# Attention and two-layer network on one Trainium2 core: units from 18 on scored in three chunks of 128 keys and a shared rest of 64

## Chip, core and metric

The kernel runs on one core of one Trainium2 chip. The metric is device time in microseconds from start to end of one execution; several executions are timed and the median is given. The profile is one more execution, recorded by the hardware profiler.

The engines of the core: TensorE (PE; its weight loads are listed apart as PEld), VectorE (DVE), ScalarE (ACT), GpSimd (POOL) and SyncE (SP). GpSimd and SyncE also issue the DMAs here, each in the order of its own queue. Each engine runs its instructions in program order, and semaphores hold it where it needs another's result.

## The reference

```python
batch, n_heads, seq, head_dim = (8, 12, 448, 64)
n_tokens, d_model, d_ff = (3584, 768, 2048)

scores = scale * np.matmul(q, k.transpose(0, 1, 3, 2))
scores = scores - np.max(scores, axis=-1, keepdims=True)
attn = np.exp(scores)
attn = attn / (np.sum(attn, axis=-1, keepdims=True) + 1e-09)
attn_out = np.matmul(attn, v)

x = attn_out.transpose(0, 2, 1, 3).reshape(B * S, H * D)
h = x @ w_in
g = np.maximum(0.01 * h, h)
out = g @ w_out
```

Inputs and output are float32; the kernel computes in bfloat16 with float32 sums.

## The kernel before

**Units, chunks, bursts.** Attention is cut into `NU` = 48 *units*: a unit is one batch and a pair of heads. A unit's 448 keys are cut into `NSC` = 4 *chunks* of `SC` = 112 keys. The scores of a chunk (`scores`, L284) are two matmuls, one for each head of the pair: 64 rows (the head dimension) of the array each, on the upper and the lower half of the rows, with the keys as weights and all 448 queries as the moving operand. They fill a *slot*, two banks of PSUM; there are three (`slots`). ScalarE turns a slot into exponentials in `e_sb` (`expo`, L296), 896 a partition; no maximum is taken off. A *burst* (`burst`, L819) is the scores of the next three chunks, whatever units they belong to, one slot each, and their exponentials.

**Rows.** When a unit's four chunks are there, `rows` (L790) multiplies by v: for each head and each 112 queries, four matmuls with the exponentials as weights and 65 columns of v moving (64 and a column of ones, which gives the sum), 32 in all, into one slot. VectorE takes the reciprocal of the sums and multiplies; x is then turned by a transposing DMA on SP's queue (or, for the units in `X_PE`, by TensorE) into `xT`.

**The supply of a unit.** GpSimd issues the loads of q, k and v, two units at a time, with a cast to bfloat16 on the way (`load_soft`, L140); the loads use rooms in not yet used weight buffers first, then `ld_pool` with two buffers a kind. GpSimd then copies q and k of a unit into one of four `qkb` buffers and v into one of four `v_sb` buffers (`cast`, L165). Up to unit 14 (`NPE` = 15) TensorE transposes q and k (`transposes`, L265); from unit 15 on one transposing DMA on SP's queue does it (`dma_transposes`, L257), into one of `NQ` = 4 buffers `qkT`. SP's queue also carries the turns of x (`x_transposes`, L320) and all stores of the output.

**The network.** Tokens are cut at `cuts` into seven blocks. For each block come the hidden layer (`hidden`, L464, matmuls L489; for the first block `head` and `neck`) and the output layer (`second` with `block_pair`, L544, matmuls L561). Both use a scheme that replaces eight half-size products by seven, with sums and differences on VectorE (`mix_x_part`, `mix_h` and others).

**The order.** Python writes out the whole order of the instructions. During `head`, `neck` and `second`, `place` (L878) decides after every few products what to put between them: a transpose, a burst, or a unit's rows. It has a small model of time: `model["now"]` for TensorE, `model["act"]` for ScalarE, when each slot comes free, when each unit's exponentials are ready. `plan` (L875) says how many bursts each of the seven `second` stages takes; `need` says how many units must be done for each block. During `hidden` two of the three slots serve the products, no burst is placed, and the loop at L999 puts rows at every fourth step. `advance` (L768) issues turns, copies and loads as their lookahead allows (a turn of unit u when `u < chunk // NSC + NQ`, a copy when `u < to["turn"] + 2`); `feed` (L857) does that in the first block.

Of the kernel before, what the change touches and what calls it, by code (L numbers as in the profile page):

```python
# [16 lines left out]
def kernel(  # L17
# [9 lines left out]
    nc = tc.nc  # L27
# [10 lines left out]
    NU = B * HP  # L38
    scale = 1.0 / float(D) ** 0.5
# [10 lines left out]
    ld_pool = ctx.enter_context(tc.tile_pool(name="ld", bufs=2))  # L50
# [32 lines left out]
    v_sb = [v_pool.tile([SC, 2, NSC, VL], BF16, name=f"v{i}") for i in range(NV)]  # L83
# [3 lines left out]
    e_sb = [exp_pool.tile([SC, EL + P - SC], BF16, name=f"e{i}") for i in range(NE)]  # L87
# [4 lines left out]
    qkT = [qk_pool.tile([P, QL + P - SC], BF16, name=f"qkT{i}") for i in range(NQ)]  # L92
# [27 lines left out]
    qkb = [cast_pool.tile([SC, 2, NSC, 2, D], BF16, name=f"qkb{i}") for i in range(4)]  # L120
# [4 lines left out]
    for t, n in ((h_mix, 2), (w_in_mix, 9), (w_mix, 9)):  # L125
        t = t.rearrange("p x k n -> p (x k n)")
        for j in range(n):
            rooms.append(t[:SC, ts(j, 4 * NSC * D)].bitcast(F32).rearrange("p (h so d) -> p h so d", h=2, so=NSC))

    def room(x):  # L130

        return rooms.pop(0) if rooms else ld_pool.tile([SC, 2, NSC, D], F32, name="f" + "qkv"[x])

    def half(t, i=None):

        t = t.rearrange("p h so d -> p (h so d)").bitcast(BF16)
        t = t.rearrange("p (u h so d) -> p u h so d", u=2, h=2, so=NSC)
        return t if i is None else t[:, i]

    def load_soft(u, n, which):  # L140
        b, hp = divmod(u, HP)
        for x in which:
            t = room(x)
# [8 lines left out]
    def load_one(u, x, queue):  # L152
        b, hp = divmod(u, HP)
        t = room(x)
# [10 lines left out]
    def cast(u, parts=(0, 1, 2), by=nc.gpsimd.tensor_copy):  # L165
        if u >= NU:
            return
        for x in parts:
            f = raw[u].pop(x)
            if x < 2 and u not in qk_sb:  # L170
                qk_sb[u] = qkb[u % len(qkb)]
            t, n = (qk_sb[u][:, x], D) if x < 2 else (v_sb[u % NV], D)
            if f.dtype == BF16 and by == nc.gpsimd.tensor_copy:
                t, f, n = t.bitcast(F32), f.bitcast(F32), D // 2
            by(t.rearrange("p so h d -> p h so d") if x < 2 else t[:, :, :, :n], f)  # L175
# [60 lines left out]
    for t in e_sb:  # L236
        nc.vector.memset(t[:, EL:], 0.0)
    for t in qkT:
        nc.vector.memset(t[:, QL:], 0.0)
# [14 lines left out]
    def turn(dst, src):  # L254
        nc.sync.dma_start_transpose(out=dst.rearrange("p (c s) -> p c s", s=SC), in_=src)
# [9 lines left out]
    def transposes(u, bank=None):  # L265
        if u >= min(NPE, NU):
            return
        for parts in ((1,), (0,)) if u == 0 else ((0, 1),):
            tr = turn_tile(bank)
            for i in parts:  # L270
                for so in range(NSC):
                    nc.tensor.transpose(  # L272
                        tr[:, i, ts(so, SC)], qk_sb[u][:, i, so], ident[:SC, :SC]
# [9 lines left out]

# [751 lines left out]
```

## Time and profile before

| | |
|---|---|
| median of 3 runs | 383.2 us (383.15 to 383.98) |
| the profiled execution, its own time | 382.9 us |
| its span, first to last instruction | 381.1 us |
| instructions | 10099 |
| mean granted clock of TensorE | 1.000 |
| score matmuls (L289), 64 rows x 448 columns | 384 |
| exponentials (L298), 112 x 896 | 192 |
| attention times v in `rows` (L799), 112 rows x 65 columns | 1344 |
| output-layer matmuls of 384 columns (L561): with w_out and h, w_mix and h, w_mix and h_mix | 448, 216, 112 |
| loads of q, k, v in `ld_pool` (two units each) | 19 each |
| transposing DMAs of q and k, of x | 33, 44 |
| DMA packets, moved | 92798, 46.98 MB |

How such lines are read: a group is "line engine op, out<-in, shapes xcount | busy us, mean ns of one | idle time of the engine just before them, and what ended most of it". A wait is "engine, line <- what it waited for: us in total, times, longest". A timeline row is "start us, us, engine line op, tiles, shapes xcount", several like instructions merged. A window row is "from:to length, busy (xcount) ..., granted clock, DMA share, GB/s". Matmul ends are modelled, so TensorE is best read from start to start.

### The profile page before, as it was taken

How to read it: one execution, taken by the hardware profiler on the slowest of the kernel's cores; microseconds unless marked ns; L12 is line 12 of the kernel's file. 1: busy time of each engine (PE TensorE's matmuls, PEld its weight loads, DVE VectorE, ACT ScalarE, POOL GpSimd, SP SyncE). 2: the span in 40 equal slices, each digit the busy share in tenths (PEclk: the TensorE clock that was granted, in tenths of full speed). 3: DMA queues.
4: the chain of work that ended last, by engine and by line, in shares of the span. 5: the costliest groups of instructions: out<-in, count | busy, mean ns of one | idle time of the engine just before them, and what ended most of it. 6: DMA issues, size and time to landing. Idle time of an engine off the chain costs nothing.

```text
span 381.1 us, 10099 instructions
## 1 busy us (share of the span) xinstructions
PE 374.3 (98%) x4123; PEld 261.4 (69%) x4123; DVE 232.1 (61%) x510; ACT 265.1 (70%) x392; POOL 111.7 (29%) x223
## 2 busy tenths in 40 slices
PE   8899999999999999999999999999999999999996
PEld 6665658756598565986558865688656895668854
DVE  3662767776666645666466674665745665474753
ACT  6997885866768777588766777668777687717700
POOL 5966663452326211251121512213322000000000
PEclk9999999999999999999999999999999999999999
DMA  8999999999898945999458994679949630331023
GB/s 157 168 202 203 200 190 207 181 124 168 133 179 81 139 108 99 165 112 123 118 89 148 107 144 89 118 131 99 159 71 147 122 61 0 109 77 33 1 83 84
DMA packets 92798, 46.98 MB, mean 123 GB/s; under 512 B 51408, under 2 KB 89424, under 8 KB 92752
## 3 DMA queue, kind: packets, MB, share of 16 engines
q0 software_dynamic: 37536, 22.24, 45.6%
q1 hardware_dynamic: 54480, 23.44, 35.5%
q10 hardware_dynamic: 736, 0.66, 0.6%
q8 instruction: 32, 0.52, 0.6%
q14 instruction: 14, 0.11, 0.1%
HBM read 45.61 MB, written 11.01 MB: 149 GB/s over the span
## 4 chain that ended last, share of the span: by engine, by line
PE 94%; ACT 2%; DVE 2%; DMA 1%; issue 0%; DVEq 0%
PE g L561 34%; PE g L489 14%; PE sc L489 14%; PE sc L289 11%; PE sc L799 10%; PE g L370 4%; ACT e L298 2%; PE g L656 2%; PE g L272 1%; DMA hmix<-in_k_dram 1%; PE g L308 1%; PE sc L370 1%; DVE x L806 1%; PE g L335 0%; DVE qkT L278 0%
## 5 line engine op out<-in xcount | busy, mean ns | idle before, releaser
L298 ACT ACTIVATE e<-sc 112x896 bf16<-112x896 f32 x192 | 162.6, 920 | 45.2 <-PE sc L289 45.0
L561 PEld LDWEIGHTS <-h 128*128 128x128 bf16 x680 | 61.2, 98 | 48.0 <-issue 14.1
L561 PE MATMUL g<-w_out_sb,h 128*128 128x384 bf16 x448 | 87.2, 327 | 0.0
L478 ACT ACTIVATE h<-c 128x512 bf16<-128x512 f32 (+1 forms) x72 | 43.5, 611 | 24.0 <-DVE c L504 14.0
L489 PEld LDWEIGHTS <-w_in_sb 128*128 128x128 bf16 x576 | 54.3, 98 | 6.0
L289 PE MATMUL sc<-qkT 64*128 64x448 bf16 x384 | 50.0, 353 | 1.7 <-ACT e L298 0.6
L175 POOL COPY v<-fv 112x256 f32<-112x256 f32 x38 | 16.2, 425 | 117.3 <-PE sc L799 98.6
L799 PEld LDWEIGHTS <-e 112*128 112x128 bf16 x1344 | 46.5, 97 | 4.4
L799 PE MATMUL sc<-v,e 112*128 112x65 bf16 x1344 | 47.7, 193 | 0.0
L489 PEld LDWEIGHTS <-w_in_mix 128*128 128x128 bf16 x432 | 41.1, 98 | 4.1
L566 DVE COPY o<-g 128x384 f32<-128x384 f32 x53 | 29.4, 554 | 22.5 <-PE g L561 22.2
L561 PE MATMUL g<-w_mix,h 128*128 128x384 bf16 (+1 forms) x224 | 41.8, 325 | 0.0
L289 PEld LDWEIGHTS <-qkT 64*128 64x128 bf16 x384 | 15.8, 94 | 28.9 <-issue 19.6
L569 DVE TENSOR_TENSOR o<-o,g 128x384 f32<-128x384 f32 x42 | 23.2, 552 | 18.1 <-PE g L561 16.3
L805 DVE RECIPROCAL rec<-sc 112x8 f32<-112x8 f32 x42 | 8.7, 208 | 36.9 <-PE sc L799 36.7
L806 DVE TENSOR_TENSOR x<-sc,rec 112x512 bf16<-112x512 f32 x42 | 29.0, 691 | 1.5
L489 PE MATMUL g<-xT,w_in_sb 128*128 128x256 bf16 (+1 forms) x216 | 28.5, 268 | 0.0
L489 PE MATMUL sc<-xT,w_in_sb 128*128 128x256 bf16 (+1 forms) x216 | 28.5, 268 | 0.0
L175 POOL COPY qkb<-fq 112x256 f32<-112x256 f32 x38 | 16.7, 441 | 32.8 <-DMA fq<-in_q_dram 32.8
L175 POOL COPY qkb<-fk 112x256 f32<-112x256 f32 x38 | 17.4, 458 | 27.5 <-DMA fk<-in_k_dram 27.5
L561 PE MATMUL g<-w_mix,hmix 128*128 128x384 bf16 x112 | 21.7, 327 | 0.0
L489 PE MATMUL g<-x_mix,w_in_mix 128*128 128x256 bf16 (+1 forms) x144 | 19.0, 268 | 0.0
(107 smaller groups left out, 455.0 us busy)
## 6 DMA issues: line engine op xcount, KB each, us to landing
fq<-in_q_dram POOLq DMA_DIRECT2D x19, 224.0 KB, 7.5
fk<-in_k_dram POOLq DMA_DIRECT2D x19, 224.0 KB, 8.9
fv<-in_v_dram POOLq DMA_DIRECT2D x19, 224.0 KB, 6.0
w_in_sb<-in_moe_w_in_dram POOLq DMA_DIRECT2D x4, 768.0 KB, 12.2
w_out_sb<-in_moe_w_out_dram POOLq DMA_DIRECT2D x4, 768.0 KB, 17.9
out_dram<-o SPq DMA_DIRECT2D x7, 336.0 KB, 3.0
out_dram<-o SPq DMA_DIRECT2D x8, 288.0 KB, 3.3
out_dram<-o SPq DMA_DIRECT2D x7, 240.0 KB, 2.9
```

Source lines behind the costliest of these rows:

```text
L175: by(t.rearrange("p so h d -> p h so d") if x < 2 else t[:, :, :, :n], f)
L289: nc.tensor.matmul(ps[:, j, :S], t[j * D:(j + 1) * D, S + c * SC:S + c * SC + P], t[j * D:(j + 1) * D, :S], start=True, stop=True,)
L298: nc.scalar.activation(e[:, :, c, :], sc_t.pop((u, c))[:SC, :, :S], AX.Exp, scale=scale)
L370: nc.tensor.matmul(open_t[m][:, :n], w_in_sb[:, kk, ts(m, P)], xT[:, kk, at:at + n], start=(fresh and kk == kks[0]), stop=(kk == KD - 1),)
L478: nc.scalar.activation(hs[:, m:m + 2, cols], x.rearrange("p (m t) -> p m t", m=2), AX.Prelu, alpha=0.01)
L489: nc.tensor.matmul(ps[:, j * nh:(j + 1) * nh], w[:, kk, ts(j, P)], x[:, kk], start=(first and j == 0 and kk == 0), stop=(kk == KH - 1), sk ...
L561: nc.tensor.matmul(ps[:, cols], x[:, m], w[:, m], start=(first and m == 0), stop=(m == MH - 1), skip_group_check=True,)
L566: by(o[:, at], ps[:, :NW])
L569: nc.vector.tensor_add(o[:, at], o[:, at], ps[:, :NW])
L799: nc.tensor.matmul(ps[:, j, qc, :D + 1], e[:, at:at + P], vt[:, j, c, :D + 1], start=(c == 0), stop=(c == NSC - 1),)
L805: nc.vector.reciprocal(rec, ps[:SC, :, :, D:D + 1])
L806: nc.vector.tensor_mul(x_t[u].rearrange("p q j d -> p j q d"), ps[:SC, :, :, :D], rec.to_broadcast([SC, 2, NSC, D]))
```

## The change

From unit 18 on (`WIDE = 3 * HP`) a unit's keys are cut into three chunks of 128 and 64 left over. A burst is then the three chunks of one unit. The 64 keys left over of both heads share one matmul, the *rest* (`rest`): the weights are 128 rows (the two heads' 64 dimensions) by 128 columns (64 keys of each head), with zeros where a head's rows meet the other head's keys; the moving operand is q of both heads; the exponentials are one instruction of 448. A rest takes a slot of its own, and is placed by `place` or, in the hidden-layer stages, in the place of rows.

`rows` becomes, for each 112 queries, three matmuls a head over 128 keys, and one over the shared rest whose moving operand is v of both heads, 130 columns: 28 matmuls a unit.

To hold this, q, k and v buffers get 128 partitions; k and v loads of these units become three DMAs, with memsets that set the zeros in the buffers' first use; the transposing DMA takes 128 rows in place of 112 (q with zero rows). `qkb` has three buffers for four, so a copy waits for the turn of three units before; in `feed` a copy is put off until that turn stands in the program (unit 17's comes behind unit 14's). In the hidden-layer stages a turn is issued at most at every sixth step. `plan` goes from 46 bursts to 36.

```diff
+    WIDE = 3 * HP
+    NWC = S // P
+    REST = S - NWC * P
...
-    qkT = [qk_pool.tile([P, QL + P - SC], BF16, name=f"qkT{i}") for i in range(NQ)]
+    qkT = [qk_pool.tile([P, 2 * NSC * P], BF16, name=f"qkT{i}") for i in range(NQ)]
+    qkb = [cast_pool.tile([P, 2 * NSC, 2, D], BF16, name=f"qkb{i}") for i in range(3)]
...
+    def load_wide(u, x):
...
+        src = (q, k, v)[x][b, 2 * hp:2 * hp + 4]
+        nc.gpsimd.dma_start(
+            out=t[:, :, :, :NWC].rearrange("p u h so d -> p (u h) (so d)"),
+            in_=src[:, :NWC * P].rearrange("h (p so) d -> p h (so d)", so=NWC),
+        )
+        for j in range(2):
+            own, other = (slice(y * REST, (y + 1) * REST) for y in (j, 1 - j))
+            if u < WIDE + 4:
+                nc.gpsimd.memset(t[other, :, j, NWC], 0.0)
+            nc.gpsimd.dma_start(out=t[own, :, j, NWC], in_=src[j::2, NWC * P:].rearrange("u r d -> r u d"))
...
     def load_soft(u, n, which):
...
+            if x > 0 and u >= WIDE:
+                load_wide(u, x)
+                continue
...
     def cast(u, parts=(0, 1, 2), by=nc.gpsimd.tensor_copy):
...
+                assert u < len(qkb) or u - len(qkb) in gone, u
...
+            if x == 0 and WIDE <= u < WIDE + len(qkb):
+                nc.gpsimd.memset(qk_sb[u][96:, :NSC], 0.0)
...
+            if x == 2 and WIDE <= u < WIDE + NV:
+                for j in range(2):
+                    nc.gpsimd.memset(v_sb[u % NV][(1 - j) * REST:(2 - j) * REST, j, NWC, D:D + 1], 0.0)
...
         if NPE <= u < NU:
-            turn(qkT[u % NQ][:, :QL], qk_sb[u].rearrange("p i so h d -> p (i so h d)"))
+            gone.add(u)
+            rows_of, s = (P, P) if u >= WIDE else (SC, SC)
+            turn(qkT[u % NQ][:, :2 * NSC * s], qk_sb[u][:rows_of].rearrange("p so h d -> p (so h d)"), s)
...
+    def rest(u):
+
+        ps = next_slot()[:, 0, :S]
+        nc.tensor.matmul(ps, qkT[u % NQ][:, (2 * NSC - 1) * P:2 * NSC * P], q_of(u), start=True, stop=True)
+        at = 2 * NWC * S
+        nc.scalar.activation(e_sb[u % NE][:, at:at + S], ps, AX.Exp, scale=scale)
...
-    def advance(hold=False, due=NU):
+    def advance(hold=False, due=NU, turns=True):
...
-        if u < min(NU, chunk // NSC + NQ, to["cast"]) and (u <= due or not hold):
+        if turns and u < min(NU, scored() + NQ, to["cast"]) and (u <= due or not hold):
...
             for qc in range(NSC):
+                b, y = divmod(2 * qc, NSC)
+                for j in range(2):
+                    for c in range(NWC):
+                        at = (j * NWC + c) * S + qc * SC
+                        nc.tensor.matmul(
+                            ps[:, b, y + j, :D + 1], e[:, at:at + P], vt[:, j, c, :D + 1],
+                            start=(y + j + c == 0), stop=False, skip_group_check=True,
+                        )
+                at = 2 * NWC * S + qc * SC
+                nc.tensor.matmul(
+                    ps[:, b, y:y + 2, :D + 1], e[:, at:at + P], vt[:, :, NWC, :D + 1],
+                    start=False, stop=True, skip_group_check=True,
+                )
...
     def burst(lazy=0):
...
+        if todo[0][0] >= WIDE:
+            assert todo[0][1] == 0
+            owed_rest.append(todo[0][0])
...
-        if r < 3 or g >= NPE:
+        if (r < 3 or g >= NPE) and (u < len(qkb) or u - len(qkb) in gone):
...
-    plan = [9, 8, 8, 8, 8, 5, 0]
+    plan = [8, 7, 6, 6, 6, 3, 0]
...
-            if want > done and state < 2 and turned(last) and not blocked and len(slots) == 3 and all(
+            if want > done and state < 2 and turned(last) and not blocked and not owed_rest and len(slots) == 3 and all(
...
+            if calm and owed_rest and at[0] <= now + 0.05:
+                t = slots[0]
+                u = set_rest()
+                model["act"] = max(model["act"], now + 0.25) + 0.5
+                free[id(t)] = model["act"] + 0.15
+                ready[u] = model["act"] + 0.1
+                model["now"] = now + 0.19
+                continue
...
         for step, _ in enumerate(hidden(i)):
-            advance()
-            if step % 4 == 2 and (i > 1 or step > 2) and NSC * (rows_done + 1) <= chunk:
+            advance(turns=step % 6 == 0)
+            if step % 4 == 2 and owed_rest:
+                set_rest()
+            elif step % 4 == 2 and (i > 1 or step > 2) and rows_done < scored():
                 rows()
```

More of the change, by code (lines that the diff above doesn't have):

```diff
@@ L119 @@
     qk_sb = {}
-    qkb = [cast_pool.tile([SC, 2, NSC, 2, D], BF16, name=f"qkb{i}") for i in range(4)]
+    gone = set()
     rooms = []
@@ L153, in load_one @@
         b, hp = divmod(u, HP)
-        t = room(x)
+        t = room(x)[:SC]
         queue.dma_start(
@@ L921, in place @@
             u = to["pe"]
-            if first and full and state == 0 and u < min(NPE - 1, to["cast"] - 1) and u <= chunk // NSC + 1 and model["act"] <= now + 0.6:
+            if first and full and state == 0 and u < min(NPE - 1, to["cast"] - 1) and u <= scored() + 1 and model["act"] <= now + 0.6:
                 transposes(u)
@@ L948, in second @@
                 if x % 4 == 0:
-                    advance(i + 1 < NR and rows_done >= need[i + 2] - 3 and not all(summed), (chunk + 3 * left - 1) // NSC)
+                    advance(i + 1 < NR and rows_done >= need[i + 2] - 3 and not all(summed), at_chunk(chunk + 3 * left - 1)[0])
                 if c or x:
```

106 lines of the change are left out of this document (69 added, 37 removed).

## The prediction

> **What bounds the kernel now.** I read the page first (busy time, slices, chain), then TensorE's timeline and stage windows, and last the queues that feed it.
>
> ```profile
> PE 374.3 (98%) x4123; PEld 261.4 (69%) x4123; DVE 232.1 (61%) x510; ACT 265.1 (70%) x392; POOL 111.7 (29%) x223
> ```
> ```profile
> PE 94%; ACT 2%; DVE 2%; DMA 1%; issue 0%; DVEq 0%
> ```
>
> TensorE is busy 98% of the span and makes 94% of the chain that ends last. The waits of its matmuls ask whether that is real work or waiting on others:
>
> ```profile
> PE sc L289 <- ACT e L298: 0.6, 2, 0.4
> ```
> ```profile
> PEld L289 <- DMA qkT<-qkb: 0.6, 2, 0.3
> ```
>
> In the whole span the score matmuls (L289) waited 0.6 us for a score slot and 0.6 us for turned q and k. So the time is a sum of TensorE's matmuls, and what the change does to that sum is the forecast, provided that nothing late gets in front of it. The rows that price its pieces are from the first stage after the second token block:
>
> ```profile
> 131.71 0.49 PE L561 MATMUL g<-w_out_sb,h 128*128 128x384 bf16 x2
> 132.03 0.81 PE L561 MATMUL g<-w_mix,hmix 128*128 128x384 bf16 x4
> 132.78 0.74 PE L289 MATMUL sc<-qkT 64*128 64x448 bf16 x6
> 133.45 0.82 PE L561 MATMUL g<-w_mix,hmix 128*128 128x384 bf16 x4
> 134.11 0.49 PE L561 MATMUL g<-w_out_sb,h 128*128 128x384 bf16 x2
> 134.44 1.14 PE L799 MATMUL sc<-v,e 112*128 112x65 bf16 x32
> 135.41 1.14 PE L561 MATMUL g<-w_out_sb,h 128*128 128x384 bf16 x6
> ```
>
> The second column of a merged row holds the tail of its last matmul, so prices are read from start to start. Rows of attention times v (L799) cost 135.41 - 134.44 = 0.97 us for 32 matmuls, and the products beside them (L561) 0.163 us each: six of them fill the usual 0.98. Ahead of the burst the four from 132.03 take 0.75 instead of 0.65, and the burst itself 0.67. A burst thus costs more than its own row. Two stages with the same products and the same attention rows give its full price; the windows are of all TensorE, then of L289, L799 and L561 alone:
>
> ```profile
> 124.19:152.65 28.46, 28.46 (x291) 1.00 0.72 114
> 314.73:340.73 26.00, 26.00 (x272) 1.00 0.20 49
> ```
> ```profile
> 124.19:152.65 28.46, 5.93 (x48) 1.93 (x48) 1.00 0.72 114
> 314.73:340.73 26.00, 3.71 (x30) 1.11 (x30) 1.00 0.20 49
> ```
> ```profile
> 124.19:152.65 28.46, 4.55 (x128) 4.44 (x128) 1.00 0.72 114
> 314.73:340.73 26.00, 4.55 (x128) 4.44 (x128) 1.00 0.20 49
> ```
> ```profile
> 124.19:152.65 28.46, 20.36 (x112) 9.91 (x111) 1.00 0.72 114
> 314.73:340.73 26.00, 19.73 (x112) 10.16 (x112) 1.00 0.20 49
> ```
>
> Both have 112 products and 128 attention-times-v matmuls, and TensorE has no gap in either (the last three numbers of a row are the granted clock, the mean share of the DMA engines and GB/s). The first has 48 score matmuls, the second 30: three bursts more, and 2.46 us more. A burst therefore costs 0.82 us. Clock 1.00 throughout, so no term hangs on the clock.
>
> **The change, part by part.** Units 18 to 47 are 30 units. Before, they take four chunks each, 120 chunks, 40 bursts of three. Afterwards each takes one burst and one rest, so 30 bursts. The plan's sum falls accordingly, from 46 to 36.
>
> Removed: 10 bursts x 0.82 = **-8.2 us**.
>
> Added: 30 rests, each one matmul of 128 rows, 128 columns of weights and 448 moving columns. The nearest row has exactly this shape, w_in against 448 tokens:
>
> ```profile
> 35.04 1.14 PE g L370 x6
> ```
>
> 1.14 / 6 = 0.19 us, so 30 x 0.19 = **+5.7 us**. Lower end: nothing shows 448 columns cheaper, so 0.19. Upper end: a burst's three pairs stream 3 x 0.19 = 0.57 of its 0.82, which leaves 0.25 for passing from whole-array matmuls to 64-row ones and back; a rest that paid all of it would cost 0.44, or 7.5 us more over 30. I take 0.19, because the rest uses all 128 rows as the products do, and L799 to L561 changes weights and slots with no loss. If a rest comes right behind a burst, it only takes over the exit that the next product paid.
>
> The Trainium skill, "TensorEngine Tiling (Array Packing)", Key Properties, says that changing the tiling mode drains TensorE. That fits the 0.25 of a burst, and would put nothing on a rest. The Trainium skill, "TensorE: Matmul & The Clock Gate", Back-to-back issue gap, gives a sustained 81 ns a matmul at 128 columns and 131 ns at 512. By it a rest would cost about 0.12 (an estimate between those two figures), and the sum would be 2 us lower. The row of the same shape has 0.19, and the row decides.
>
> Attention times v: per unit 32 matmuls of 65 columns become 24 of 65 and 4 of 130, the same 2080 columns. Below, a price by instruction: 28 x 30.3 ns = 0.85 us, -0.12 a unit or -3.6 in all. Above, a price by column alone: 0.97, no gain. The two rows between which it lies, 65 columns at 30.3 ns and 448 at 190, give 0.417 ns a column and a fixed 3.2 ns. Then 130 columns take 57.4 ns, and the unit 24 x 30.3 + 4 x 57.4 = 957 ns. I take that: 0.013 x 30 = **-0.4 us**. Contracting 128 rows for 112 changes no column count.
>
> On ScalarE a unit's exponentials go from four of 896 to three of 896 and one of 448:
>
> ```profile
> L298 ACT ACTIVATE e<-sc 112x896 bf16<-112x896 f32 x192 | 162.6, 920 | 45.2 <-PE sc L289 45.0
> L634 ACT ACTIVATE h<-g 128x448 bf16<-128x448 f32 x14 | 7.7, 550 | 2.1 <-PE g L370 1.7
> ```
>
> 162.6 / 192 = 0.85 us, so 3.39 becomes 2.54 + 0.55 at most: 0.3 us less a unit. ScalarE idles 45 us in front of the exponentials waiting for scores, so this is worth nothing, but it removes a cover that could have failed. Score slots are used five times a unit before (four chunks, one rows) and after (three, the rest, one rows). The planner now counts a rest at 0.5 on ScalarE, about that price. In the hidden-layer stages, where one slot is left, a rest goes two products after the stage's start and pushes the rows back by four products (some 2.6 us); those rows are for a later token block. Cost on the path: nothing.
>
> Loads: each k and v load of two units becomes three issues on GpSimd's queue, and the first two of each kind also get two memsets.
>
> ```profile
> L144 POOL DMA_DIRECT2D fk<-in_k_dram x19 | 13.4, 704 | 2.7 <-DMA w_out_sb<-in_moe_w_out_dram 1.9 <-DMA w_in_sb<-in_moe_w_in_dram 0.5 <-issue 0.3
> ```
> ```profile
> POOL v L175 <- PE sc L799: 98.6, 22, 10.0
> ```
> ```profile
> fk<-in_k_dram POOLq DMA_DIRECT2D x19, 224.0 KB, 8.9
> ```
> ```profile
> 0.74 0.20 POOL masks.py:197 MEMSET c<- 128x128 bf16 x1 [0.29 <-POOLq L1019]
> ```
>
> Four more issues a pair of units are 4 x 0.70 = 2.8 us, 42 us over 15 pairs, and the 19 memsets at 0.2 another 4. GpSimd works 111.7 of 381 us and spends 98.6 more waiting for v buffers, which covers it. Bytes grow by nothing, but a load's pieces grow from 448 (112 partitions x 4 heads) to 512 + 256, so a k load lands in 8.9 us if bytes count and in 8.9 x 768/448 = 15.3 if pieces do. I take 12; two buffers of a pair each last four units, which is 32 us at the 8.1 us a unit worked out below, so either end is covered.
>
> The transposing DMA of q and k takes 128 rows for 112:
>
> ```profile
> L255 SPq DMA_TRANSPOSE qkT<-qkb x33: 1222/1319/3394, 60.0 to 303.9; - x33
> ...
> DMA to landing us min/median/max: 3.6/4.9/10.5
> ```
>
> At 128/112 that is 1.3 to 1.5 us on SP's queue and 4.9 to 5.6 us to landing, 30 times. SP's queue also carries the turns of x and the stores, so all of these move back by up to 0.2 us per turn. What stands between this and TensorE is slack, and it is thinnest at the end of the same stage:
>
> ```profile
> 136.48 0.74 PE L289 MATMUL sc<-qkT 64*128 64x448 bf16 x6
> ...
> 149.69 0.74 PE L289 MATMUL sc<-qkT 64*128 64x448 bf16 x6
> ```
> ```profile
> 141.98 1.88 SPq L255 DMA_TRANSPOSE qkT<-qkb  x1
> 143.98 6.82 SPq L255 DMA_TRANSPOSE xT<-x  x4
> ```
>
> The turn of unit 26 may go once the burst at 136.48 has read unit 22; it stands behind x turns and stores until 141.98, lands 4.9 later at 146.9, and is wanted at 149.69: 2.8 us of slack after 13.2 us of lookahead. With one unit a burst, six or seven bursts in about 28 us, unit u+4 is turned behind the rest of unit u and wanted four bursts later: 4 x 4.0 to 4.6 less some 2 us until the rest, 14 to 16 us. The lookahead does not shrink, so the cost is nothing.
>
> Three copied buffers for four: the copy of unit u waits for the turn of u-3 instead of u-4. Behind it on GpSimd stand v copies and load issues.
>
> ```profile
> 152.65:172.94 20.29, 20.29 (x234) 1.00 1.08 137
> ```
> ```profile
> 72.65 0.56 PE L272 MATMUL sc<-c,qkb 112*128 112x112 bf16 x8
> ...
> 88.32 0.74 PE L289 MATMUL sc<-qkT 64*128 64x448 bf16 x6
> ```
>
> A product stage and the hidden-layer stage behind it, 28.46 + 20.29 us, feed six units, 8.1 us each, and three buffers give 24 us against copy 0.8, SP's wait of up to 6.8 and landing 5.6. Covered. Unit 17's copy goes to just behind unit 14's turn, the transposes at 72.65; its first chunk is in the burst at 88.32, 15 us later, so that costs nothing either. The extra memsets before the first scores are hidden by the first loads.
>
> Sum: -8.2 + 5.7 - 0.4 = **-2.9 us**. The profiled execution took 382.9 us (span 381.1 and 1.8 around it), so 380.0; the median of the runs, 383.2, is 0.3 above that execution, so the forecast is **380.3 us**.
>
> **The rivals.**
>
> *Late q and k (slower).* Place: the score bursts at the end of the four large wide stages. Mechanism: GpSimd's 2.8 us a pair, loads of short pieces and copies that wait for the turn of u-3 put the copies back; the turn then starts late behind x turns. It decides from the point at which more than the 2.8 us of slack is eaten, less the 0.7 by which the turn lands later: 2.1. Late by 2.8 it costs 0.7 a stage; with a landing at the row's 10.5 instead of 4.9 it costs 5.6 - 2.1 = 3.5. Four stages: 2.8 to 14 us on 380.3, so 383.1 to 394.3, about 387 in the middle. For it: k loads that land in up to 15.3 us, and a DMA share that is 1.08 in the hidden-layer stage already, where packets queue. Against: the lookahead of 14 to 16 us, and a share of 0.72 in the product stage. The Trainium skill, "DMA: Bandwidth & Descriptors", Specifications, sets 512 B as the least transfer for line rate, below which the engine reads, modifies and writes; it speaks for this rival, and no load in this trace is cut that small.
>
> *The rest pays for its place (no change).* If each rest costs the 0.10 us that the products ahead of a burst show, 30 x 0.10 = 3.0 takes the gain: 383.3. Paying the full 0.25 gives 380.3 + 7.5 = 387.8. For it: no row shows one lone matmul set between two groups of products; against: the whole-array shape.
>
> *Attention times v goes by instruction (more gain).* -3.6 for -0.4: 377.1. Against: the 448-column row shows that columns count.
>
> *The change does not shorten the path.* The planner places the rests where slots are not free, TensorE waits 0.1 us at each, and the time again stays near 383. Against: 0.6 us of such waits now, and less ScalarE work.
>
> **How the numbers follow.** Forecast 0.62, more gain 0.08, no change by either route 0.13, late q and k 0.12, rests at full price 0.05. A change of 0.2%, 0.8 us, is about what the measurement tells from none. Forecast and more gain are faster: 0.70. The two no-change routes 0.13 are same. Late q and k and dear rests are slower: 0.17. The range reaches down to 377.1, the bound of the v part, and up to 385.0, which takes in no change and the light end of late q and k; that leaves out less than 2 in 10. The forecast's own range is 379 to 382.
>
> **What would show it.** Right: 324 score matmuls of 64 rows where 384 stood (18 x 8 + 30 x 6), 30 single ones of 128 x 448 at 0.19 start to start, 28 v matmuls a unit in 0.96, stages of two token blocks with six bursts at 28.46 - 2 x 0.82 + 6 x 0.19 - 0.05 = 27.9, and waits of TensorE for turned q and k still under 1 us. Wrong: TensorE's row for these waits at several us, slices of PE below 9 between 100 and 330 us, a gap ahead of each rest, or v rows of 0.85.

## The result and the profile after

The changed kernel takes 382.4 us in the median of its runs (382.18 to 383.18) beside 383.27 for the kernel before: a ratio of 0.9977 with an interval of 0.9966 to 0.9987, some 0.9 us faster. A second set of executions gave 382.70 and 0.9983 (0.9971 to 0.9996). One later execution of the changed kernel took 1325.68 us and one of rows_later 390.93; the medians and ratios here leave them out. The forecast was 380.3: the direction came, and less than a third of the 2.9 us; 382.4 lies outside the forecast's own 379 to 382 and inside the wide range of 377.1 to 385.0. The profiled execution took 382.59 us with a span of 380.8.

The first lines of the page and the list of TensorE's waits answer to the two that stand first in the prediction. First the engines' busy time and the shares of the chain, then the waits (us in total, times, longest):

```profile
PE 372.5 (98%) x3972; PEld 261.8 (69%) x3973; DVE 231.5 (61%) x513; ACT 253.2 (67%) x392; POOL 152.5 (40%) x302
...
PE 94%; ACT 2%; DVE 2%; issue 1%; DVEq 0%
```
```profile
PE g L258 <- PEq L1124: 0.8, 1, 0.8
PE sc L337 <- DVE xT L396: 0.7, 1, 0.7
PE sc L337 <- ACT e L351: 0.6, 2, 0.4
PE g L621 <- DVE o L626: 0.5, 1, 0.5
```

TensorE has 151 fewer records of matmuls and still makes 94% of the chain; the weight loads' 0.6 us of waits for turned q and k are gone. Two of the new rows name VectorE: a score pair (L337) waits for the copy of turned x (L396), and a product (L621) for the copy that empties a product bank (L626), the PSUM bank that the output layer's products fill. Before, no product and no score matmul waited for either.

**Stage by stage.** From the first product stage (73.04 us before, 73.13 after) to the end of the last matmul (377.57 and 376.76) TensorE takes 304.53 and 303.63 us, 0.90 less. (The span is only 0.3 shorter in this profile: what follows the last matmul took 4.03 us, against 3.55 before and 3.49 in the changed kernel's repeat.) Each entry is from a stage's first matmul to the next one's; the last column puts the forecast's prices (burst 0.82, rest 0.19, a unit's attention times v 0.97 before and 0.957 after) on what the stage now holds.

| stage | before | after | difference | by the forecast's prices |
|---|---|---|---|---|
| first product stage | 30.86 | 31.36 | +0.50 | 1 burst less, 2 rests: -0.44 |
| first hidden-layer stage | 20.29 | 20.26 | -0.03 | -0.03 |
| second product stage and hidden | 48.75 | 50.16 | +1.41 | 1 burst less, 7 rests, 1 unit's rows more: +1.39 |
| third and hidden | 48.74 | 48.24 | -0.50 | 2 bursts less, 6 rests, six units' rows: -0.58 |
| fourth and hidden | 48.78 | 48.25 | -0.53 | -0.58 |
| fifth and hidden | 44.27 | 43.75 | -0.52 | -0.58 |
| sixth product stage | 26.00 | 24.77 | -1.23 | 2 bursts less, 3 rests, 1 unit's rows less: -2.08 |
| all that follows | 36.84 | 36.84 | 0 | 0 |

The column sums to -0.90, the forecast's to -2.9. Between the second and the fifth product stage every stretch is within 0.08 of its forecast. The gain is lost in two places: 0.94 in the first product stage and 0.85 in the sixth. The stage windows of both kernels, before and then after (length, then busy time of TensorE, its weight loads, VectorE, ScalarE and GpSimd, each with its count, the clock, DMA share, GB/s), of the first, third and sixth product stage:

```profile
73.04:103.90 30.86, 30.70 (x335) 17.36 (x333) 21.34 (x48) 21.90 (x27) 13.45 (x26) 1.00 1.18 145
172.94:201.39 28.45, 28.45 (x290) 16.09 (x288) 15.96 (x37) 21.34 (x27) 5.54 (x13) 1.00 0.65 106
```
```profile
73.13:104.49 31.36, 30.52 (x331) 17.33 (x327) 21.75 (x50) 22.27 (x28) 20.69 (x50) 1.00 1.09 135
174.91:201.92 27.01, 27.01 (x241) 15.08 (x238) 17.07 (x40) 18.98 (x27) 11.86 (x24) 1.00 0.70 105
315.15:339.92 24.77, 24.23 (x219) 14.43 (x218) 14.56 (x31) 10.33 (x16) 0.00 (x0) 1.00 0.18 47
```

The third is full (27.01 of 27.01). The first and the sixth have gaps of 0.84 and 0.54 that were 0.16 and, by the prediction's row, none.

**The prices themselves** are what the forecast said. TensorE's timeline of the changed kernel at a rest in the second product stage (start, length, operation), and at a unit of attention times v:

```profile
136.23 1.15 PE L621 MATMUL g<-w_out_sb,h 128*128 128x384 bf16 x6
137.22 0.35 PE L356 MATMUL sc<-qkT 128*128 128x448 bf16 x1
137.41 1.46 PE L621 MATMUL g<-w_mix,h 128*128 128x384 bf16 x8
138.80 0.74 PE L337 MATMUL sc<-qkT 64*128 64x448 bf16 x6
```
```profile
330.08 0.34 PE L888 MATMUL sc<-v,e 128*128 128x65 bf16 x6
...
331.04 1.79 PE L621 MATMUL g<-w_out_sb,h 128*128 128x384 bf16 x10
```

The rest (L356) goes from 137.22 to 137.41, 0.19 us. The eight products behind it take 1.39, of which 0.09 is the time ahead of the burst at 138.80 that each burst had before. Attention times v goes from 330.08 to 331.04, 0.96 us for 28 matmuls.

**The first place: the end of the first product stage.** TensorE's timeline there, the changed kernel:

```profile
97.31 0.35 PE L356 MATMUL sc<-qkT 128*128 128x448 bf16 x1
...
97.90 1.15 PE L877 MATMUL sc<-v,e 112*128 112x65 bf16 x32
...
100.14 0.37 PE L395 MATMUL sc<-c,x 112*128 112x112 bf16 x4
...
100.78 0.55 PE L337 MATMUL sc<-qkT 64*128 64x448 bf16 x4
102.04 0.36 PE L337 MATMUL sc<-qkT 64*128 64x448 bf16 x2 [0.72 <-DVE xT L396]
```

Unit 18's rest, and two products behind it, now stand ahead of unit 17's attention times v (L877), and unit 17's x is turned on TensorE (L395) at 100.14, for 99.30 before. Turned x lies in a score slot until VectorE has copied it out, and the burst's third pair wants that slot. VectorE's timeline over the same time, before and after:

```profile
99.63 0.55 DVE L569 TENSOR_TENSOR o<-o,g 128x384 f32<-128x384 f32 x1
100.09 0.39 DVE L336 COPY xT<-sc 128x448 bf16<-128x448 bf16 x1
100.39 0.42 DVE L434 TENSOR_TENSOR x_mix<-xT 128x512 bf16<-128x512 bf16 x1
```
```profile
100.47 0.42 DVE L494 TENSOR_TENSOR x_mix<-xT 128x512 bf16<-128x512 bf16 x1
100.81 0.55 DVE L629 TENSOR_TENSOR o<-o,g 128x384 f32<-128x384 f32 x1
101.27 0.42 DVE L494 TENSOR_TENSOR xT<-xT 128x512 bf16<-128x512 bf16 x1
101.61 0.38 DVE L396 COPY xT<-sc 128x448 bf16<-128x448 bf16 x1
```

Before, the copy comes ahead of the differences of x (L434); after, two differences (L494), already due while the copy was not yet, come ahead of it. Two pairs of a burst take 0.45, so the third pair was due at 101.23; it goes at 102.04, when the copy is done.

**The second place: the sixth product stage.** TensorE's timeline of the changed kernel, then VectorE's:

```profile
329.10 1.14 PE L621 MATMUL g<-w_out_sb,h 128*128 128x384 bf16 x6
...
333.37 1.46 PE L621 MATMUL g<-w_mix,h 128*128 128x384 bf16 x8 [0.54 <-DVE o L626]
```
```profile
331.31 0.21 DVE L899 RECIPROCAL rec<-sc 112x8 f32<-112x8 f32 x1 [1.45 <-PE sc L893]
331.56 0.69 DVE L900 TENSOR_TENSOR x<-sc,rec 112x512 bf16<-112x512 f32 x1
332.16 0.68 DVE L633 TENSOR_TENSOR h<-h 128x1024 bf16<-128x1024 bf16 x1
332.76 0.55 DVE L626 COPY o<-g 128x384 f32<-128x384 f32 x1
```

The last unit's attention times v (330.08 to 331.04 above) was placed after six of the eight products that fill a bank. Before, a burst (329.64) stood among these products, and attention times v came after ten of them (331.30); two bursts less leave none there. So VectorE had the other order before:

```profile
331.17 0.69 DVE L573 TENSOR_TENSOR h<-h 128x1024 bf16<-128x1024 bf16 x1 [1.52 <-PE g L561]
331.78 0.55 DVE L566 COPY o<-g 128x384 f32<-128x384 f32 x1
332.54 0.21 DVE L805 RECIPROCAL rec<-sc 112x8 f32<-112x8 f32 x1 [0.21 <-PE sc L799]
```

Now the reciprocal and multiplication take VectorE from 331.31 to 332.16, and the difference of h (L633) and the copy that empties the product bank (L626) stand behind them. The ten products from 331.04 are over by 331.04 + 10 x 0.163 = 332.67; the next goes at 333.37, 0.70 late.

### The profile page after: what moved, and what is told of

Read it like the earlier page. It is cut to its first block, busy times and chain, and to the rows that moved or that the text cites. A ratio compares the mean times of both kernels' runs of the same rounds, so it can differ in the third digit from the quotient of the medians.

```text
span 380.8 us, 9900 instructions
## 1 busy us (share of the span) xinstructions
PE 372.5 (98%) x3972; PEld 261.8 (69%) x3973; DVE 231.5 (61%) x513; ACT 253.2 (67%) x392; POOL 152.5 (40%) x302
## 2 busy tenths in 40 slices
DMA packets 107198, 47.95 MB, mean 126 GB/s; under 512 B 79248, under 2 KB 103824, under 8 KB 107152
## 4 chain that ended last, share of the span: by engine, by line
PE 94%; ACT 2%; DVE 2%; issue 1%; DVEq 0%
PE g L621 34%; PE sc L549 14%; PE g L549 14%; PE sc L337 9%; PE sc L888 6%; PE g L430 4%; PE sc L877 3%; PE g L716 2%; ACT e L351 2%; PE sc L893 2%; PE sc L356 1%; PE g L258 1%; PE g L314 1%; PE g L368 1%; PE sc L430 1%
## 5 line engine op out<-in xcount | busy, mean ns | idle before, releaser
L351 ACT ACTIVATE e<-sc 128x896 bf16<-128x896 f32 (+1 forms) x162 | 137.4, 922 | 42.4 <-PE sc L337 42.2
L621 PEld LDWEIGHTS <-h 128*128 128x128 bf16 x680 | 62.8, 98 | 50.2 <-issue 12.8
L621 PE MATMUL g<-w_out_sb,h 128*128 128x384 bf16 x448 | 86.5, 327 | 0.0
L337 PE MATMUL sc<-qkT 64*128 64x448 bf16 x324 | 42.8, 353 | 2.4 <-DVE xT L396 0.7
L626 DVE COPY o<-g 128x384 f32<-128x384 f32 x53 | 29.4, 555 | 24.3 <-PE g L621 24.2
L209 POOL COPY v<-fv 128x256 f32<-128x256 f32 (+1 forms) x38 | 15.2, 407 | 71.7 <-PE sc L893 47.5
L621 PE MATMUL g<-w_mix,h 128*128 128x384 bf16 (+1 forms) x224 | 41.9, 324 | 0.5 <-DVE o L626 0.5
L888 PEld LDWEIGHTS <-e 128*128 128x128 bf16 x720 | 30.4, 97 | 3.5 <-ACT e L351 2.3
L888 PE MATMUL sc<-v,e 128*128 128x65 bf16 x720 | 32.1, 193 | 0.0
L209 POOL COPY qkb<-fq 112x256 f32<-112x256 f32 x38 | 16.6, 436 | 38.6 <-DMA fq<-in_q_dram 20.3
L337 PEld LDWEIGHTS <-qkT 64*128 64x128 bf16 x324 | 12.8, 94 | 25.6 <-issue 18.3
L900 DVE TENSOR_TENSOR x<-sc,rec 112x512 bf16<-112x512 f32 x42 | 29.0, 691 | 1.5
L893 PE MATMUL sc<-v,e 128*128 128x130 bf16 x120 | 26.7, 222 | 0.0
L209 POOL COPY qkb<-fk 128x256 f32<-128x256 f32 (+1 forms) x38 | 18.7, 493 | 16.0 <-DMA fk<-in_k_dram 16.0
L621 PE MATMUL g<-w_mix,hmix 128*128 128x384 bf16 x112 | 23.3, 326 | 0.0
```

The lines of the kernel that those rows point to most:

```text
L337: nc.tensor.matmul(ps[:, j, :S], t[j * D:(j + 1) * D, k0:k0 + P], q_of(u)[j * D:(j + 1) * D] if u >= WIDE else t[j * D:(j + 1) * D, :S], s ...
L351: nc.scalar.activation(e[:, :, c, :], sc_t.pop((u, c))[:e.shape[0], :, :S], AX.Exp, scale=scale)
L621: nc.tensor.matmul(ps[:, cols], x[:, m], w[:, m], start=(first and m == 0), stop=(m == MH - 1), skip_group_check=True,)
L626: by(o[:, at], ps[:, :NW])
L888: nc.tensor.matmul(ps[:, b, y + j, :D + 1], e[:, at:at + P], vt[:, j, c, :D + 1], start=(y + j + c == 0), stop=False, skip_group_check=True,)
L893: nc.tensor.matmul(ps[:, b, y:y + 2, :D + 1], e[:, at:at + P], vt[:, :, NWC, :D + 1], start=False, stop=True, skip_group_check=True,)
```

## The experiments

The reason tested is that the gain of the forecast is real and is given back at these two places (seams, in the expectations: the two-seams theory); by the every-unit theory each of the 30 units lacks a little instead. The other rivals are those of the prediction (a rest that costs more in its place, attention times v by instruction, late q and k) and, later, that GpSimd's added work slows VectorE. Times are medians with the ratio to the kernel before, run beside each set (383.06 to 383.42), and its interval.

**The first place mended (x_first).** The first part of the next block's differences of x too waits until turned x is copied.

```diff
-  if fresh[y] is not None and fresh[y] <= model["now"] and not summed[y] and not (y and owed_x):
+  if fresh[y] is not None and fresh[y] <= model["now"] and not summed[y] and not owed_x:
```

> Only the order on VectorE around unit 17's x changes: the differences of x for the next block wait until the turned x is copied out of its slot. Two-seams theory: the 0.72 us wait of the third score pair of unit 19 for that copy shrinks to 0.2 or less, the first product stage goes from 31.36 to 30.5 to 30.7, and the time falls by 0.6 to 0.9 us against the changed kernel, to about 381.7. It could be taken back if the differences then come too late for the hidden-layer stage. Every-unit theory: the time stays within 0.2 us of the changed kernel.

381.78 us, 0.9960 (0.9947 to 0.9974). The first product stage takes 30.69 for 31.36, and no wait for L396 is left. (The fourth and fifth took 27.19 and 27.20 in this execution, 0.18 more: in each a product waits for its bank, at 225.99 and 274.41, behind a difference of h that took 0.95 for 0.69. The last experiments take such stretched instructions up.) VectorE's timeline, with the addition and the copy first again:

```profile
100.22 0.55 DVE L629 TENSOR_TENSOR o<-o,g 128x384 f32<-128x384 f32 x1
100.69 0.38 DVE L396 COPY xT<-sc 128x448 bf16<-128x448 bf16 x1
100.99 0.41 DVE L494 TENSOR_TENSOR x_mix<-xT 128x512 bf16<-128x512 bf16 x1
```

**The second place mended (rows_later).** No attention times v may go after the first six products of a pair of token blocks of 128; only the last unit's moves, two products on.

```diff
...
-  if calm and whole and not (lazy and late) and at[0] <= now + 0.05 and ready.get(u, 0) <= now + 0.05 and (
+  if calm and apart and whole and not (lazy and late) and at[0] <= now + 0.05 and ready.get(u, 0) <= now + 0.05 and (
...
-  left -= place(i, left, calm=x not in (1, 2), keen=need[min(i + 2, NR)], cap=NU if all(summed) else need[i + 2])
+  left -= place(i, left, calm=x not in (1, 2), apart=x != 3, keen=need[min(i + 2, NR)], cap=NU if all(summed) else need[i + 2])
```

> Only unit 47's rows move, two products later, behind the copy of the first output product. Two-seams theory: the 0.70 us that TensorE waits for that copy near 333 us goes, the last wide product stage falls from 24.77 to about 24.1, and the time by 0.6 to 0.8 us against the changed kernel. Every-unit theory: within 0.2 us of the changed kernel.

382.19 us, 0.9974 (0.9964 to 0.9985). The sixth product stage takes 24.09 for 24.77, and so it does, within 0.01, in all five profiles with this place mended. VectorE's timeline shows the difference of h and the bank's copy ahead of the reciprocal:

```profile
331.93 0.69 DVE L633 TENSOR_TENSOR h<-h 128x1024 bf16<-128x1024 bf16 x1 [0.74 <-PE g L621]
332.54 0.55 DVE L626 COPY o<-g 128x384 f32<-128x384 f32 x1
333.00 0.20 DVE L899 RECIPROCAL rec<-sc 112x8 f32<-112x8 f32 x1
```

The profiled execution shows a first product stage of 32.43, though, longer than the changed kernel's 31.36 with the same code there; the last experiments take that up.

**The changed kernel again (after_again), and both places mended (both_seams, both_again).**

> The changed kernel once more, beside the three that follow. Both theories: 0.8 to 1.0 us faster than the kernel before, last matmul of TensorE 0.8 us earlier. Two-seams theory: the stretches between the seams (stages two to four, a product stage with the hidden-layer stage behind it) 0.5 us shorter each, the first product stage 0.9 too long and the last wide one 0.85 too long against the sum. Every-unit theory: the missing 2.0 us would show as 0.07 us a unit in each of the 30 units, so these stretches would be 0.1 us shorter each.

> Both of these edits together. Two-seams theory: the gains add, 1.2 to 1.7 us against the changed kernel, about 380.9 us, 2.1 to 2.6 us faster than the kernel before, near the sum of 2.9. Every-unit theory: within 0.3 us of the changed kernel, about 382.2.

> The kernel with both seams mended, once more, beside the others of this call. Theory (two seams cost the changed kernel what its forecast lacked): 381.0 to 382.2 us, 0.995 to 0.997 of the kernel before, first product stage 30.7, last wide product stage 24.1. Rival (the gain in the earlier profile was one lucky execution): a median of 382.3 or more, first product stage 31.4 or more.

The changed kernel again: 382.70 us, 0.9983 (0.9971 to 0.9996), with a first product stage of 31.88. Both mended: 381.91, 0.9959 (0.9946 to 0.9973), and in the repeat 381.7, 0.9958 (0.9941 to 0.9975). So about 1.6 us under the kernel before, where the change alone gave 0.6 to 0.9; the 2.1 to 2.6 expected of both mended did not come in the medians. In the repeat's profile the first product stage took 31.22, nearer to the rival's 31.4 than to 30.7; a subtraction was stretched there, which the last experiments take up. In the first of the two profiles the first product stage takes 30.69 and the sixth 24.09, and the stretch to the last matmul 302.25, 2.28 less than before's 304.53. The two places thus account for 0.67 + 0.68 = 1.35 of the 2.0 us that TensorE's work was short of the forecast. Of the other 0.6, 0.27 stays in the first product stage, 0.17 in the sixth and 0.05 to 0.08 in each of the three wide stretches between.

Part of this can be read from the trace, though no run changed it alone. Once in each stage from the first to the fifth, the first weight load of a unit's attention times v waits up to 0.29 us for an exponential, by the order of the slots the one that frees the slot which it is to fill, and its first matmul starts 0.07 late. The list of TensorE's weight loads has this as a new row (`PEld L888 <- ACT e L351: 2.3, 9, 0.3`). In the first product stage a burst's third pair also starts 0.17 late, at 93.30, right behind VectorE's multiplication (L900), which ends at 93.25.

**Attention times v by column or by instruction (v_split).** The matmul of 130 columns is cut into two of 65.

```diff
-  nc.tensor.matmul(
-      ps[:, b, y:y + 2, :D + 1], e[:, at:at + P], vt[:, :, NWC, :D + 1],
-      start=False, stop=True, skip_group_check=True,
-  )
+  for j in range(2):
+      nc.tensor.matmul(
+          ps[:, b, y + j, :D + 1], e[:, at:at + P], vt[:, j, NWC, :D + 1],
+          start=False, stop=True, skip_group_check=True,
+      )
```

> The changed kernel with each 130-column matmul over the shared rest cut in two of 65 columns, so 32 matmuls a unit again, over 128 rows. Price by column with a fixed 3.2 ns: a unit's rows go from 0.96 to 0.97 us, the time up by 0.4 us to 382.8. Price by instruction: 4 x 30.3 ns more a unit, the rows from 0.85 or what they are to 0.12 more, the time up by 3.6 us to 386.

382.88 us, 0.9992 (0.9982 to 1.0001). The stage table decides: the third to fifth product stages take 27.04, 27.04 and 27.03 for 27.01, and the hidden-layer stages 21.26 for 21.23, so 0.01 us for each unit's four added matmuls, as the 0.013 worked out from a price by column. By instruction it would have been 0.12.

**The price of a rest (rest_twice).** Each rest's matmul is issued twice into the same slot.

```diff
-  nc.tensor.matmul(ps, qkT[u % NQ][:, (2 * NSC - 1) * P:2 * NSC * P], q_of(u), start=True, stop=True)
+  for _ in range(2):
+      nc.tensor.matmul(ps, qkT[u % NQ][:, (2 * NSC - 1) * P:2 * NSC * P], q_of(u), start=True, stop=True)
```

> The changed kernel with the matmul of each rest issued twice into the same slot. Rest priced as its row: 0.19 us a rest, 30 x 0.19 = 5.7 us, about 388.1, product stages with six rests 1.1 us longer. If a rest also paid for its place, the second one would not pay it again, so the first would show start to start as 0.29 or more; two-seams theory: 0.19 for each.

387.29 us, 1.0110 (1.0093 to 1.0127). The second product stage goes from 28.94 to 30.15, 1.21 for seven, and the third from 27.01 to 28.04, 1.03 for six: 0.17 each, and the time is less than the 388.1 expected. TensorE's timeline shows the pair:

```profile
181.27 0.54 PE L357 MATMUL sc<-qkT 128*128 128x448 bf16 x2
181.65 1.46 PE L622 MATMUL g<-w_mix,h 128*128 128x384 bf16 x8
```

Two take 0.38, and one 0.19 as it stands: the first costs no more than the second. A rest pays nothing for its place.

**Late q and k (loads_twice).** Each short load of left-over keys is issued twice.

```diff
-  nc.gpsimd.dma_start(out=t[own, :, j, NWC], in_=src[j::2, NWC * P:].rearrange("u r d -> r u d"))
+  for _ in range(2):
+      nc.gpsimd.dma_start(out=t[own, :, j, NWC], in_=src[j::2, NWC * P:].rearrange("u r d -> r u d"))
```

> The changed kernel with each of the two short loads of the keys left over issued twice, 60 more issues on GpSimd, 35 us of its time, with the packets that go with them. Supply hidden, as forecast: the product and hidden-layer stages from the second block on keep their lengths within 0.1 us, and the waits of TensorE for turned q and k stay under 1 us. Supply late: these waits rise to 1 us or more a stage, the time to 386 or more. If GpSimd's work stretches VectorE's where the two are busy together, the first product stage (73 to 104 us) alone grows, by 0.3 to 1 us.

506.75 us, 1.323 (1.32 to 1.3257), at a granted clock of 0.892: far from what was expected. The edit added a wait, not only work, as the waits of TensorE and of GpSimd show (two views of the same kernel):

```profile
PE sc L338 <- DMA qkT<-qkb: 102.0, 11, 13.5
```
```profile
POOL fv L164 <- DMA fv<-in_v_dram: 96.8, 30, 5.6
POOL fk L164 <- DMA fk<-in_k_dram: 95.6, 30, 11.6
```

The second load into the same place is issued only when the first has landed, 60 times with a mean of 3.2 us in which GpSimd's queue stands still. The copies behind it and the turns behind those come late, and TensorE waits 102 us for turned q and k. The run therefore prices no load. It shows the prediction's slow rival as it looks when it does decide, in the row of TensorE's waits that is absent from the changed kernel, and that GpSimd's slack is less than the 192 us / 15 = 12.8 us a pair of units added here.

**The buffers and the turns alone (three_buffers, turns_free).** The kernel before with three buffers of copied q and k and the copy of unit 17 behind unit 14's turn; and the changed kernel with turns at every step of the hidden-layer stages.

```diff
-  qkb = [cast_pool.tile([SC, 2, NSC, 2, D], BF16, name=f"qkb{i}") for i in range(4)]
+  qkb = [cast_pool.tile([SC, 2, NSC, 2, D], BF16, name=f"qkb{i}") for i in range(3)]
...
-  if r < 3 or g >= NPE:
+  if (r < 3 or g >= NPE) and (u < len(qkb) or u - len(qkb) in gone):
```
```diff
-  advance(turns=step % 6 == 0)
+  advance()
```

> The kernel before with one part of the change alone: three buffers of copied q and k, and a copy put off until the turn of three units before stands in the program. Forecast: costs nothing, 383.3 within 0.3 us, the product stages of two token blocks 28.46 us as before. If the third buffer were what is missing, 1 us or more slower, with waits for turned q and k.

> The changed kernel with the turns of q and k in the hidden-layer stages issued at any step instead of every sixth. The forecast's view (lookahead of 14 to 16 us, queue of SP with slack): the same as the changed kernel within 0.3 us, 382.4 to 382.9, waits of TensorE for turned q and k under 1 us either way. Rival (the spacing of turns carries part of the gain, since x turns and stores would stand behind them): 0.5 us or more slower.

Three buffers: 383.58 us, 1.0011 (1.0001 to 1.0021), with stages of 30.85, 28.46, 28.56, 28.46, 28.46 and 26.01: at most 0.11 us in one stage. Free turns: 382.13 us, 0.9964 (0.9950 to 0.9977), a little under the 382.4 to 382.9 expected, every stage within 0.02 of the changed kernel's. Neither part cost what the forecast lacks.

**GpSimd's added work (early_zeros, zeros_many).** GpSimd is busy 152.5 us for 111.7, and the first product stage varied between executions of the same code. VectorE, GpSimd and TensorE in the changed kernel's repeat, three views of nearly the same time:

```profile
76.36 1.74 DVE L451 TENSOR_TENSOR w_out_sb<-w_out_sb 128x768 bf16<-128x768 bf16 x1
...
78.25 0.69 DVE L900 TENSOR_TENSOR x<-sc,rec 112x512 bf16<-112x512 f32 x1
```
```profile
76.35 0.59 POOL L163 DMA_DIRECT2D fv<-in_v_dram  x1
76.94 0.41 POOL L209 COPY v<-fv 112x256 f32<-112x256 f32 x1
77.27 0.41 POOL L209 COPY qkb<-fq 112x256 f32<-112x256 f32 x1
77.62 0.74 POOL L209 COPY qkb<-fk 112x256 f32<-112x256 f32 x1
```
```profile
78.99 0.36 PE L337 MATMUL sc<-qkT 64*128 64x448 bf16 x2 [0.34 <-DVE x L900]
```

While GpSimd issues a load and copies without a break, the subtraction L451 takes 1.74; all four of its kind take 0.55 in the changed kernel's first profile, the last (78.31) beside copies of GpSimd too. The multiplication behind it (L900) then frees a score slot late, and a score pair waits 0.34 for it. Two kernels with both places mended test whether the amount of GpSimd's work sets this: the three memsets of copied q go to VectorE at the start, or each is issued five times.

```diff
-  if x == 0 and WIDE <= u < WIDE + len(qkb):
-      nc.gpsimd.memset(qk_sb[u][96:, :NSC], 0.0)
...
+  for t in qkb:
+      nc.vector.memset(t[96:, :NSC], 0.0)
```
```diff
-      nc.gpsimd.memset(qk_sb[u][96:, :NSC], 0.0)
+      for _ in range(5):
+          nc.gpsimd.memset(qk_sb[u][96:, :NSC], 0.0)
```

> Both seams mended, and the three memsets of 0.52 us that zero the unused rows of copied q are moved from GpSimd in the first product stage to VectorE ahead of the first copies. Theory A (VectorE's instructions stretch while GpSimd works back to back, and this varies from execution to execution in the first product stage): 1.6 us less GpSimd work there, so the median comes 0.2 to 0.6 us under the one of both seams mended, fewer stretched VectorE instructions between 74 and 86 us, first product stage 30.4 to 30.7. Theory B (the spread comes from elsewhere, where loads land): the same time within 0.2 us and the same spread.

> Both seams mended, and each of those three memsets on GpSimd is issued five times, 6.2 us more GpSimd work in the first product stage, which nothing waits for. Theory A (stretching): VectorE instructions of 1 us and more between 74 and 92 us, first product stage 31.2 to 33, median 0.5 to 2 us over the one of both seams mended. Theory B: the same time within 0.3 us, because GpSimd's queue has slack of several us there.

Less GpSimd work: 382.49 us, 0.9978 (0.9962 to 0.9994). More: 381.8, 0.9949 (0.9936 to 0.9963). That is the wrong order for the theory of an amount, which falls; the interval of both mended, 0.9941 to 0.9975, meets both. In the eleven profiles with the rests (the one with doubled loads left out) the first product stage was longer whenever one subtraction of w_out was stretched (us; in brackets its length):

| first product stage | subtraction 0.55 to 0.72 | stretched |
|---|---|---|
| first place as changed | 31.36, 31.36 | 31.88, 31.88 (1.74); 32.43 (1.05); 32.44 (1.05, with two rests doubled: 0.35 of it) |
| first place mended | 30.69, 30.69 | 31.22 (1.75), 31.10 (1.30), 30.88 (1.41) |

The stretch is not the whole of it. In the two longest a score pair already waits ahead of the stretched subtraction, 0.65 us in the profile of 32.43 (at 75.14) and 0.37 in that of 32.44: VectorE had waited 2.8 and 2.6 us there for the load of w_out, and at most 1.7 in the others. Nor is it this subtraction alone. Differences of h (L633, L639), 0.69 as a rule, took 0.85 to 1.64 somewhere behind the first product stage in nine of the eleven profiles. Most of these leave the stage's length as it was; the two in x_first are those that cost its fourth and fifth stage 0.18 each.

The kernel before (30.86) and the one with three buffers (30.85) show no stretched subtraction (0.62 at most), but the latter has a difference of h of 0.88. With one profile of each, that the change brings the stretches is not shown. What decides whether one occurs, the time at which a load lands and lets GpSimd's copies go being the candidate, stays open; no run varied that alone.

## Why the prediction was right and wrong

**Bursts removed, rests added, attention times v: right.** The wide stretches came within 0.08 of the sum made from 0.82, 0.19 and 0.957, and doubling and splitting gave 0.17 for a rest and 0.01 for the four matmuls. By the figures for back-to-back matmuls of "TensorE: Matmul & The Clock Gate" in the Trainium skill a rest was estimated at 0.12; 0.19 start to start and 0.17 by doubling decide for the row. The Trainium skill, "TensorEngine Tiling (Array Packing)", Key Properties, says that a change of tiling mode drains TensorE; the whole-array rest between whole-array products, at 0.19, agrees, as it changes no mode.

**Where the rows fall: a detail off, with no cost.** The forecast for a wide product stage was 27.9; it is 27.0, and the hidden-layer stage behind it has 21.2 for 20.3, since one more unit's attention times v went there. The pair is what was forecast.

**ScalarE: right but for little.** The score matmuls' waits for ScalarE's exponentials are 0.6 us in both kernels. New are those of the weight loads of attention times v above, which put their matmuls 0.07 us late once in a wide stage.

**Loads, turns and buffers at nothing: right.** The large part of a k load lands in 5.5 us in the median and the short parts in 5.3, not in 12 (all times from issue to landing):

```profile
fk<-in_k_dram POOLq DMA_DIRECT2D x15, 192.0 KB, 5.5
fk<-in_k_dram POOLq DMA_DIRECT2D x30, 16.0 KB, 5.3
```

So the pieces under 512 bytes that the Trainium skill ("DMA: Bandwidth & Descriptors", Specifications) warns of made nothing late here, though the profile counts 79248 packets under 512 bytes for 51408 before.

**The step that failed: the score slots, "Cost on the path: nothing".** The prediction counted that slots are used five times a unit before and after, and put the new order at nothing. It looked for delay on ScalarE and on GpSimd's and SP's queues, and did not follow VectorE, which frees slots and banks too. What it said of rows pushed back is of the hidden-layer stages, and no rest fell there: all 30 stand in product stages. Where attention times v moves among the products, that unit's reciprocal, multiplication and copy of turned x move to another place in VectorE's order, among additions, bank copies and differences whose places did not move. Where VectorE has some 0.8 us of work put ahead of an instruction that frees a slot or a bank, TensorE waits. In the wide stages between, the order falls well, and at most 0.08 us a stage is lost. At the end of the first product stage, where a rest went ahead, and in the middle of the sixth, where bursts were gone, it falls badly. Of the 0.94 and 0.85 us that these stages lack, 0.67 went away when VectorE's order alone was changed, and 0.68 when one unit's attention times v was placed two products later. VectorE's busy share of 61% does not show it.

**The rivals.** Late q and k, dear rests and the price by instruction did not come, by the runs above. "The change does not shorten the path" came nearest, in the time and in part in the mechanism: TensorE waited for a slot at one place and for a bank at the other, each for VectorE's work, and not at each rest.

**What is left.** Some 0.6 us of TensorE's time, in part read above and not tested, and first product stages that are 0.2 to 1.1 us longer in seven of eleven profiles, with a stretched subtraction in each and a late load of w_out in the two longest. The prediction had neither; the cause of the stretches is open.

## What to carry to other kernels

When a matmul is put into a tuned order, follow every instruction that it displaces to the engine that consumes its result: there the order of issue decides, and an engine that is 61% busy still holds TensorE up if one slot's release stands behind two others. A price by stage, from the first matmul of one to the first of the next, tells whether a forecast failed in its prices, everywhere a little, or in one or two stages. Mend such a place by moving one instruction and look whether that stage alone shortens, since the time of the whole may vary by as much.

## What the runs showed of the hardware

A VectorE subtraction of two 128 x 768 operands took 0.55 us as a rule and 1.05 to 1.75 in seven profiles, while GpSimd issued loads or copied without a break; other profiles have the same neighbours and no stretch (0.55 at 78.31 in the changed kernel's first). The Trainium skill, "SBUF — State Buffer", Who interferes with whom, says that VectorE and GpSimd share a pair of ports as an exclusive lock. That would allow such a stretch, and no run here shows that it is the cause. Six more us of GpSimd's memsets did not lengthen the stage, which speaks against the amount of work.

A second load into a place that was just loaded was held on GpSimd's queue until the first had landed, 3.2 us in the mean and up to 11.6.
